# A held weight load, two loads moved ahead, and a routing cut into smaller steps

## The chip, the cores and the metric

The kernel runs on one core of a Trainium2 chip. The metric is the device time of one execution in microseconds; several executions are taken and the median is given. The profile is of one execution.

## The reference: linear attention, then a top-1 mixture of experts

Eight batches of 576 tokens, eight heads of 64, are put through attention without a softmax; the 4608 rows of 512 that come out each go to one of eight experts:

```
kv  = einsum('bhsd,bhse->bhde', k, v)
out = einsum('bhsd,bhde->bhse', q, kv)
x   = out / rms(out) * g_norm                # rows of 512, N = 4608
e   = argmax(x @ w_gate)                     # one expert of 8 per row
y   = softmax(x @ w_gate)[e] * sigmoid(x @ w_output_gate)[e] * (relu(x @ w1[e]) @ w2[e])
```

Everything is float32. The kernel keeps that precision with two-part operands: each weight or activation is split into a rounded part (`whi`, `xT`, `hT` high) and a remainder (`wlo`, ...), and three matmuls take the place of one.

## The kernel before

**Stages.** Attention goes batch by batch: the state of a batch (`kvps`, from loads `ld<-kvm` in four chunks and `ld<-rem`), a projection (`kvTps`, `mps`), then tiles of 128 rows (`ops`). The first sixteen tiles are made in `early()`; the rest in `late()`, a generator whose pieces are run between the matmuls of the experts. Tiles are routed in four groups of 9, 7, 10 and 10 (`route()`): scales, argmax, a count of the rows before each row, and tables of row numbers (`tblps`, added up in `tacc`).

**Experts.** After the second group each expert has a table of its first 256 rows, and GpSimd gathers them (`xg`, the rows, and `tl`, their scales). `run(i)` is one expert run: eight column blocks of the first matmul (`mm1`, tile `hps`, 12 matmuls each at 256 columns; block f+2 uses the PSUM buffer that ScalarE and VectorE have emptied of block f into `hT`), then two row tiles of the second (`mm2`, tile `yps`, 24 matmuls of 512 columns each). Seven such runs stand beside `late()`. The other rows are gathered for eight later runs, when all four groups are routed and the experts are ordered by size (`rows_of_all`, `epos`, `gidx`).

**Order.** Each engine's instructions stand in the order in which this program writes them (a manual schedule), so an instruction that waits holds back all behind it on its engine. SyncE issues nearly all loads: weights (`wload`, 512 KB each, tile `wraw`), attention inputs (512 KB each) and row writes (`xs<-xrow`). GpSimd issues the gathers and the output scatters. A DMA also waits until the one eight places before it, which used the same semaphore, has landed.

**At the end of `early()`.** The first chunk of the first expert's w1 was loaded earlier. The other three are held by a dependency (`behind`, L217 issues them): one until the first tail gather has landed, two until the second. Behind them on SyncE stand a row write, four chunks of w2 (held until VectorE has scaled the second gathered tile), and then the loads of the sixth batch.

**In `mm2` and `late()`.** `run()` gives out routing work in two ways: `unit`, one step of `late()` after each mm1 block and at one place of each mm2 tile, and `step()` at four more places of a tile. A step of `route()` is up to six instructions, or fewer up to a `yield 1`. Before a group's table matmuls of the third and fourth group three steps are let pass.

Of the kernel before, what the change touches and what calls it, by code (L numbers as in the profile page):

```python
# [11 lines left out]
F32 = mybir.dt.float32  # L12
# [9 lines left out]
P = 128  # L22
# [6 lines left out]
NT = NTOK // P  # L29
# [122 lines left out]
def body(ctx: ExitStack, tc: tile.TileContext, kvm, rem, qT, wg, gn, w1, w2, kc, xs, xr, xt, tab, out):  # L152
    nc = tc.nc
# [126 lines left out]
            out=o[:M, :], out_offset=None, in_=dram[0:XE] if i < E else dram,  # L280
            in_offset=bass.IndirectOffsetOnAxis(ap=gidx[i // E][:M, RUNS[i][0], t:t + 1], axis=0))

    issued = []

    def gather(i, after=None):
        for t, c0, M in tiles_of(i):
            xg[(i, t)] = take([P, DM], F32, "xg")
            x_ = fetch(i, t, M, xs, xg[(i, t)])
            if after is not None and t == tiles_of(i)[0][0]:
                tc.add_manual_dep(x_.ins, after.ins.name,  # L290
                                  mybir.DependencyInfo(mybir.DependencyClass.Sync, mybir.DependencyReason.DATA),
                                  reason="order of the gathers")
            gathered = gather_tail(i, t, M, xr if i < 2 else xt)
            issued.append(gathered)
        return gathered

    def tail_of(i, k, after=None, new=False):
# [23 lines left out]
    def behind(i_, after):  # L321
        if after is not None:
            tc.add_manual_dep(i_.ins, after.ins.name,
                              mybir.DependencyInfo(mybir.DependencyClass.Sync, mybir.DependencyReason.DATA),
                              reason="pace of the gathers")
        return i_
# [373 lines left out]
    def route(gi):  # L700
# [257 lines left out]
        yield from pause(8)  # L958
        if g0 >= EARLY:

            yield 1
            yield 1
            yield 1

        def table_part(t0, t1, rl=None):
            w = t1 - t0
# [13 lines left out]
        if not early:  # L980
            tps = ps_t.tile([P, 2, E * TMAX], F32, name="tblps", tag="t")
            for t in range(n):
                nc.tensor.matmul(tps, las[t], rc[:, t, 0:2], start=(t == 0), stop=(t == n - 1))
            yield from pause(9)
            vec.tensor_tensor(out=tacc, in0=tacc, in1=tps, op=ALU.add)
        elif not lead:
            tps, acc = table_part(0, TMAX)
            yield from pause(9)
            vec.tensor_copy(acc, tps)
            scales_late.append(rest_of_scales())  # L990
        else:
            tps, acc = table_part(0, TA, rl)
            yield from pause(9)
            vec.tensor_tensor(out=gidx[0][:, :, 0:TA], in0=acc, in1=tps, op=ALU.add)
            gather(0)
            vec.tensor_tensor(out=acc, in0=acc, in1=tps, op=ALU.add)
            for _ in places(0, tacc[:, 0].rearrange("p (e t) -> p e t", t=TMAX), 0, TA):
                pass
            ea = sm.tile([P, E], F32, name="ea", bufs=1)
            vec.tensor_tensor(out=ea, in0=cf[:, K_A:K_A + E], in1=rp[:, n], op=ALU.subtract)  # L1000
            ab_ = c1.tile([P, E], BF16, name="adj")
            vec.tensor_scalar(out=ab_, in0=ea, scalar1=0.0, scalar2=None, op0=ALU.max)
            adj.append(ab_)
            for _ in tokens_so_far():
                pass
            tick[0] = None

            scales_late.append(rest_of_scales())

            def others():  # L1010
                for k in range(3):
                    marks(TA, TMAX, k)
                    yield
                tps, acc = table_part(TA, TMAX)
                yield
                vec.tensor_tensor(out=acc, in0=acc, in1=tps, op=ALU.add)

            tables_late.append(others())
# [2 lines left out]
            yield from rows_of_all()  # L1021

    scales_late, tables_late = [], []
    xwrites = []
    opened = [False]

# [29 lines left out]
                if k == 2:  # L1056
                    routing.remove(r)

    def step(n=6):

        while n and routing:
            n -= 1
            k = next(routing[0], 2)
            if k == 2:
                routing.pop(0)
            if k:
                break
# [13 lines left out]
    def early():  # L1081

        nonlocal done_tiles

        def more():
            load(loads, free)
            if not loads and not opened[0]:
                open_rows()

        w1s = list(range(4))  # L1090

        def send(n=0):
            load(early_extra[:1] and [early_extra.pop(0)], free) if n else wload(0, 1, w1s.pop(0))

        more()
        for b in range(FIRST_B - 1):
            lim = min(tiles_ready(b - 1) if b else 0, EARLY)
            kv = kv_part(b)
            for k in range(4):
                next(kv)  # L1100
                more()
                if lim - done_tiles > 2:
                    run_out(lim)
            cp = next(kv)
            more()
            if not run_out(lim):
                constants(COLD[2])
            kvT = kvT_part(cp)
            if not run_out(lim) or b == FIRST_B - 2:
                constants(COLD[2])  # L1110
            m_part(b, kvT)
            if b == FIRST_B - 2:
                constants(COLD[5])
            more()
            while run_out(lim):
                more()

        while squares:
            sums()
        lim = tiles_ready(FIRST_B - 2)  # L1120
        kv = kv_part(FIRST_B - 1)
        assert not loads
        send()
        run_out(lim)
        constants(1)
        send(1)
        send(1)
        run_out(lim)
        for k in range(4):
            next(kv)  # L1130
            if k < 3:
                advance()
            if k == 1:
                run_out(lim)
                send(1)
                send(1)
        cp = next(kv)
        advance()
        kvT = kvT_part(cp)
        evict = out_tile(done_tiles, True)  # L1140
        done_tiles += 1
        m_part(FIRST_B - 1, kvT)
        evict()
        if len(squares) > 2:
            sums()
        advance()
        constants(COLD[2])
        assert done_tiles == lim
        run_out(EARLY)
        paced[0] = False  # L1150
        while run_out(EARLY):
            constants(1)
        constants(COLD[5])
        for r in rows:
            r()
        while squares:
            constants(COLD[2], sums())
        while routing:
            advance()
            if routing and COLD[3][at_pause[0]]:  # L1160
                constants(COLD[3][at_pause[0]], tick[0])
        while early_extra:
            send(1)
        for c in w1s:
            behind(wload(0, 1, c), issued[0] if c == 1 else issued[1])
        for k in range(PIECES):
            next(rest)
        constants(COLD[4], tick[0])
# [261 lines left out]
    with tc.manual_schedule(engines=MAN):  # L1430
# [24 lines left out]
            run(i, lambda n: next(rest, None))  # L1455
        for _ in rest:
            assert False
    p1.close()
    rp_[1] = main.enter_context(tc.tile_pool(name="rb", bufs=1))
    hp = main.enter_context(tc.tile_pool(name="hp", reuse_waits="tile", bufs=1))  # L1460
# [113 lines left out]
```

## Time and profile before

| | us |
|---|---|
| median of three runs (lowest, highest) | 589.47 (588.39, 592.59) |
| profiled execution | 589.1 |
| span of its trace | 587.3 |

The span reaches from the first to the last instruction of the trace; the profiled execution took 1.8 us more. TensorE (PE) is busy for 556.2 us of the span. A share of busy time is an average over stages with different limits, so the stages have to be read one by one: where PE waits, for whom, and what that one waited for. Engines are PE (matmul), PEld (its weight loads), DVE (VectorE), ACT (ScalarE), POOL (GpSimd) and SPq (SyncE's queue).

### The profile page before, as it was taken

Reading aid. Unit: us, or ns where it says so; the run is one execution under the profiler, and the core shown is the slowest. Engines: PE = TensorE matmul, PEld = TensorE weight load, DVE = VectorE, ACT = ScalarE, POOL = GpSimd, SP = SyncE. Lnnn points to the kernel's source line nnn. Section 1 sums busy time; section 2 is a strip of 40 time slices with the busy share of each in tenths; the row PEclk is TensorE's granted clock in tenths of the full one; section 3 lists DMA queues with packets and bytes.
Section 4 is the critical chain, followed back from the end, with each engine's and each line's share of the span. In section 5 each row is a group of like instructions: output and inputs, shape, how many; then the busy total and the mean of one; then the engine's idle time right before and its main releaser. Section 6 shows DMA issues by size and latency. Waiting matters only on the chain.

```text
span 587.3 us, 11846 instructions
## 1 busy us (share of the span) xinstructions
PE 556.2 (95%) x4626; PEld 476.4 (81%) x4626; DVE 345.1 (59%) x634; ACT 285.8 (49%) x482; POOL 217.2 (37%) x202
## 2 busy tenths in 40 slices
PE   7898769999999979999999999999999999999995
PEld 3774658898988778889989879889897988888894
DVE  2268574655587999757595737446345363656450
ACT  1354445656576637456563534435445353535430
POOL 3342333331313241524484515325263443545202
PEclk9999999999999999999999999999999999999998
DMA  8999599798967572865857436346554654656201
GB/s 305 408 410 337 160 393 406 286 353 285 317 216 246 176 269 67 304 230 178 283 155 250 129 122 185 111 155 189 166 168 141 199 155 153 199 168 205 74 6 37
DMA packets 38586, 126.18 MB, mean 215 GB/s; under 512 B 6877, under 2 KB 8142, under 8 KB 38528
## 3 DMA queue, kind: packets, MB, share of 16 engines
q1 hardware_dynamic: 29520, 105.19, 52.1%
q0 software_dynamic: 8288, 19.82, 10.1%
q8 instruction: 38, 0.62, 0.4%
q10 hardware_dynamic: 720, 0.38, 0.2%
q14 instruction: 20, 0.16, 0.1%
HBM read 106.01 MB, written 19.91 MB: 214 GB/s over the span
## 4 chain that ended last, share of the span: by engine, by line
PE 77%; DMA 8%; DVE 7%; ACT 3%; issue 3%; POOL 1%; SPq 0%; POOLq 0%; ACTq 0%; DVEq 0%
PE hps L389 33%; PE yps L425 30%; PE ops L644 4%; DMA ld<-kvm 4%; PE kvps L565 3%; PE tps L345 3%; PE yps L419 3%; DVE wlo L263 2%; ACT whi L260 1%; DMA wgs<-wg 1%; DMA wraw<-w 1%; DVE wlo L256 1%; PE cps L540 1%; DMA tl<-xr,gidx 1%; DVE la L897 0%
## 5 line engine op out<-in xcount | busy, mean ns | idle before, releaser
L389 PE MATMUL hps<-xT,whi 128*128 128x256 f32 (+8 forms) x1008 | 218.2, 309 | 6.0 <-DVE hT L399 5.2
L425 PE MATMUL yps<-whi,hT 128*128 128x512 f32 (+3 forms) x592 | 199.1, 400 | 0.0
L389 PEld LDWEIGHTS hps<-xT,whi 128*128 128x128 f32 x1008 | 167.1, 190 | 12.0 <-DVE hT L399 6.0
L389 PE MATMUL hps<-xT,wlo 128*128 128x256 f32 (+8 forms) x504 | 153.4, 304 | 0.0
L425 PEld LDWEIGHTS yps<-whi,hT 128*128 128x128 f32 (+3 forms) x592 | 110.1, 186 | 24.0
L397 ACT ACTIVATE hT<-hps 128x256 fp32r<-128x256 f32 (+8 forms) x128 | 55.0, 430 | 127.1 <-PE hps L389 124.6
L425 PE MATMUL yps<-wlo,hT 128*128 128x512 f32 (+3 forms) x296 | 116.0, 392 | 0.0
L399 DVE SCALAR_TENSOR_TENSOR hT<-hps,hT 128x256 fp32r<-128x256 f32 (+9 forms) x168 | 63.0, 395 | 88.8 <-ACT hT L397 88.4
L438 POOL DMA_INDIRECT out<-y,oidx x42 | 47.2, 1124 | 181.5 <-ACT y L437 153.4
L256 DVE SCALAR_TENSOR_TENSOR wlo<-wraw,gcol,whi 128x1024 fp32r<-128x1024 f32 x62 | 83.3, 1345 | 46.3 <-ACT whi L253 46.2
L263 DVE TENSOR_TENSOR wlo<-wraw,whi 128x1024 fp32r<-128x1024 f32 x64 | 85.1, 1330 | 28.0 <-ACT whi L260 26.5
L389 PEld LDWEIGHTS hps<-xT,wlo 128*128 128x128 f32 x504 | 95.9, 190 | 0.3
L253 ACT ACTIVATE whi<-wraw,gcol 128x1024 fp32r<-128x1024 f32 x62 | 71.3, 1150 | 0.7 <-DVE wlo L263 0.7
L279 POOL DMA_INDIRECT xg<-xs,gidx x42 | 47.1, 1121 | 57.3 <-PE hps L389 38.3
L260 ACT CAST whi<-wraw 128x1024 fp32r<-128x1024 f32 x64 | 66.6, 1040 | 1.9 <-issue 1.9
L279 POOL DMA_INDIRECT tl<-xt,gidx x42 | 54.1, 1288 | 30.0 <-PE hps L389 21.4
L425 PEld LDWEIGHTS yps<-wlo,hT 128*128 128x128 f32 (+3 forms) x296 | 55.2, 186 | 10.4
L315 POOL TENSOR_TENSOR xg<-xg,tl 128x512 f32<-128x512 f32 (+8 forms) x40 | 42.9, 1071 | 51.0 <-DMA tl<-xt,gidx 42.5
L437 ACT ACTIVATE y<-yps,tl 128x512 f32<-128x512 f32 (+3 forms) x37 | 25.4, 688 | 59.9 <-PE yps L425 47.9
L348 ACT CAST xT<-tps 128x512 fp32r<-128x512 f32 (+8 forms) x42 | 23.0, 547 | 39.4 <-PE tps L345 38.4
L349 DVE TENSOR_TENSOR xT<-tps,xT 128x512 fp32r<-128x512 f32 (+8 forms) x42 | 26.8, 637 | 19.3 <-ACT xT L348 19.0
L565 PEld LDWEIGHTS kvps<-ld 128*64 128x64 f32 (+1 forms) x640 | 21.8, 139 | 15.4 <-DMA ld<-kvm 7.4
(175 smaller groups left out, 442.3 us busy)
## 6 DMA issues: line engine op xcount, KB each, us to landing
wraw<-w SPq DMA_DIRECT2D x128, 512.0 KB, 4.5
ld<-kvm SPq DMA_DIRECT2D x32, 512.0 KB, 9.7
ld<-qT SPq DMA_DIRECT2D x18, 512.0 KB, 9.0
xs<-xrow SPq DMA_DIRECT2D x18, 512.0 KB, 4.3
ld<-rem SPq DMA_DIRECT2D x4, 512.0 KB, 7.9
xg<-xs,gidx POOLq DMA_INDIRECT x42, 4.1
tl<-xt,gidx POOLq DMA_INDIRECT x42, 4.7
out<-y,oidx POOLq DMA_INDIRECT x42, 3.3
```

Source lines behind the costliest of these rows:

```text
L253: he.activation(hi, r, AF.Copy, scale=gcol[:, 0:1])
L256: eng.scalar_tensor_tensor(out=lo, in0=r, scalar=gcol[:, 0:1], in1=hi.bitcast(F32), op0=ALU.mult, op1=ALU.subtract)
L260: he.copy(hi, r)
L263: eng.tensor_tensor(out=lo, in0=r, in1=hi.bitcast(F32), op=ALU.subtract)
L279: return nc.gpsimd.indirect_dma_start(out=o[:M, :], out_offset=None, in_=dram[0:XE] if i < E else dram, in_offset=bass.IndirectOffsetOnAxi ...
L315: return eng.tensor_tensor(out=v, in0=v, in1=f, op=ALU.mult)
L389: seq.append(nc.tensor.matmul(ps[:, :C], w[:, o:o + P], x[d][:, :C], start=(d == 0 and k == 0), stop=(d == 3 and k == 2)))
L397: nc.scalar.activation(h[:, 0:C], ps[:, :C], AF.Relu)
L399: nc.vector.scalar_tensor_tensor(out=h[:, l:l + b - a], in0=ps[:, a:b], scalar=0.0, in1=h[:, a:b].bitcast(F32), op0=ALU.max, op1=ALU.subtract)
L425: seq.append(nc.tensor.matmul(ps[:M], a, b, start=(f == 0 and n == 0), stop=(f == 7 and n == 2)))
L438: i_ = nc.gpsimd.indirect_dma_start(out=out, out_offset=bass.IndirectOffsetOnAxis(ap=oidx[i // E][:M, RUNS[i][0], t:t + 1], axis=0), in_=y ...
L565: nc.tensor.matmul(ps[u * D:(u + 1) * D, p * D:(p + 1) * D], k, v, start=(s == 0 and p == 0), stop=(s == 4 and p == NP - 1))
```

## The change

Three things. The second and third chunk of the first expert's w1 are no longer held; the fourth waits for a one-column memset that GpSimd executes behind its four gather instructions, so for their issue and not for their landing. Two loads of the sixth batch go out right behind it. And routing is spread: once all tiles are made and only the last group is being routed, a step has at most three instructions, and the third group's table comes two steps later.

```diff
@@ in route()
         if g0 >= EARLY:
 
-            yield 1
-            yield 1
-            yield 1
+            for _ in range(5 if not last else 3):
+                yield 1
...
             gather(0)
+            issued.append(nc.gpsimd.memset(issue_mark, 0.0))
...
-    def step(n=6):
-
+    def step():
+
+        n = 3 if done_tiles == NT and len(routing) == 1 and not squares else 6
         while n and routing:
...
@@ in early()
         while early_extra:
             send(1)
-        for c in w1s:
-            behind(wload(0, 1, c), issued[0] if c == 1 else issued[1])
+        for c in w1s[:-1]:
+            wload(0, 1, c)
+        behind(wload(0, 1, w1s[-1]), issued[0])
+        assert len(xfree) > 2
+        load([late_loads.pop(0) for _ in range(2)], xfree)
```

**SyncE, at the end of `early()`.** `wraw<-w` is a chunk of expert weights, `ld<-kvm` a chunk of keys and values; in brackets stand the semaphores that a row waits for (DMAHW: another load, DMASW: a gather, Pool: GpSimd). Before:

```order
L530 DMA ld<-kvm 128x1024 [waits DMAHW4_49,PE_49]
L530 DMA ld<-rem 128x1024 [waits DMAHW5_49,PE_49]
L217 DMA wraw<-w 128x1024 [waits DMAHW6_49,DMASW4_49,PE_49]
L217 DMA wraw<-w 128x1024 [waits DMAHW7_49,DMASW6_49,PE_49]
L217 DMA wraw<-w 128x1024 [waits DMAHW0_49,PE_49]
L1031 DMA xs<-xrow 128x1024 [waits DMAHW1_49,Activation_49]
L217 DMA wraw<-w 128x1024 [waits DMAHW2_49,DVE_49,PE_49]
```

Now:

```order
L528 DMA ld<-kvm 128x1024 [waits DMAHW4_49,PE_49]
L528 DMA ld<-rem 128x1024 [waits DMAHW5_49,PE_49]
L217 DMA wraw<-w 128x1024 [waits DMAHW6_49,PE_49]
L217 DMA wraw<-w 128x1024 [waits DMAHW7_49,PE_49]
L217 DMA wraw<-w 128x1024 [waits DMAHW0_49,PE_49,Pool_49]
L528 DMA ld<-kvm 128x1024 [waits DMAHW1_49]
L528 DMA ld<-kvm 128x1024 [waits DMAHW2_49]
L1031 DMA xs<-xrow 128x1024 [waits DMAHW3_49,Activation_49]
L217 DMA wraw<-w 128x1024 [waits DMAHW4_49,DVE_49,PE_49]
```

The two waits for gathers are gone, one for GpSimd is new, and two loads have come from behind the w2 chunks to in front of them. The semaphores of all later loads shift by two places with them: the sixth batch's third and fourth chunk had to wait for the first and second w2 chunk (DMAHW2, DMAHW3), and now wait for its second chunk and the row write.

**VectorE, in the mm1 of the fifth expert run.** `hT` is VectorE's part of emptying a block, `wlo` the split of a w2 chunk, the others are routing of the last group (`tacc`: the third group's table). From the first block's `hT`, before:

```order
L399 SCALAR_TENSOR_TENSOR hT<-hps,hT 128x256 [waits Activation_49]
L734 SCALAR_TENSOR_TENSOR ru<-ry 128x80 [waits DVE_49]
L736 TENSOR_TENSOR ru<-ru,ss 128x80 [waits DVE_49]
L738 SCALAR_TENSOR_TENSOR xtail<-ru,ry 128x10x8 [waits DVE_49]
L399 SCALAR_TENSOR_TENSOR hT<-hps,hT 128x256 [waits Activation_49]
L263 TENSOR_TENSOR wlo<-wraw,whi 128x1024 [waits DMAHW3_49,Activation_49]
L749 TENSOR_TENSOR gp<-gp,xtail 128x10x64 [waits DVE_49]
L749 TENSOR_TENSOR gp<-gp,xtail 128x10x64
L399 SCALAR_TENSOR_TENSOR hT<-hps,hT 128x256 [waits Activation_49]
```

Now:

```order
L397 SCALAR_TENSOR_TENSOR hT<-hps,hT 128x256 [waits Activation_49]
L982 TENSOR_TENSOR tacc<-tacc,tblps 128x96 [waits PE_49]
L397 SCALAR_TENSOR_TENSOR hT<-hps,hT 128x256 [waits Activation_49]
L263 TENSOR_TENSOR wlo<-wraw,whi 128x1024 [waits DMAHW3_49,Activation_49]
L717 TENSOR_SCALAR ry<-ss 128x80
L724 SCALAR_TENSOR_TENSOR ru<-ry 128x80 [waits DVE_49]
L726 TENSOR_TENSOR ru<-ru,ss 128x80 [waits DVE_49]
L397 SCALAR_TENSOR_TENSOR hT<-hps,hT 128x256 [waits Activation_49]
L728 SCALAR_TENSOR_TENSOR ru<-ru 128x80 [waits DVE_49]
L730 SCALAR_TENSOR_TENSOR ry<-ru,ry 128x80 [waits DVE_49]
L397 SCALAR_TENSOR_TENSOR hT<-hps,hT 128x256 [waits Activation_49]
```

Eight small instructions of the last group that stood ahead of the second block's `hT` stand two to three ahead of each, and the rest of that group's work comes later by as much; its argmax (`ohb`), which stood ahead of the fifth block's `hT`, now stands ahead of the eighth's.

**PE, second row tile of the fourth expert run.** `tps` are transposes of gathered rows, `tblps` the third group's table, each of its matmuls on a freshly loaded `la`. Before:

```order
L345 MATMUL tps<-ident,xg 128x128 x3
L425 MATMUL yps<-whi,hT 128x512
L425 MATMUL yps<-wlo,hT 128x512
L425 MATMUL yps<-whi,hT 128x512
L983 LDWEIGHTS la [waits DVE_49]
L983 MATMUL tblps<-rrc,la 128x96 [waits PE_49]
```

Now, from the `yps` behind the transposes:

```order
L423 MATMUL yps<-whi,hT 128x512
L423 MATMUL yps<-wlo,hT 128x512
L423 MATMUL yps<-whi,hT 128x512 x2
L423 MATMUL yps<-wlo,hT 128x512
L423 MATMUL yps<-whi,hT 128x512 x2
L423 MATMUL yps<-wlo,hT 128x512
L423 MATMUL yps<-whi,hT 128x512 x2
L423 MATMUL yps<-wlo,hT 128x512
L423 MATMUL yps<-whi,hT 128x512 x2
L423 MATMUL yps<-wlo,hT 128x512
L423 MATMUL yps<-whi,hT 128x512
L980 LDWEIGHTS la [waits DVE_49]
```

The table has moved behind twelve matmuls of the tile, to its end. The last group's table moved likewise, from the fifth run's second row tile into the sixth run's mm1.

## Rows read from the trace of the kernel before

**Rows 1.** the page's head; then by stage: stretch, engines' busy time, PEclk, DMA share, GB/s

```profile
span 587.3 us, 11846 instructions
...
56.00:66.00 10.00, 8.31 (x168) 5.41 (x166) 6.03 (x29) 3.04 (x7) 5.05 (x6) 1.00 0.52 145
78.00:94.00 16.00, 10.64 (x154) 9.45 (x153) 10.83 (x27) 7.75 (x17) 3.77 (x4) 0.89 1.03 407
94.00:176.00 82.00, 82.00 (x1010) 70.64 (x1008) 50.78 (x80) 51.76 (x95) 25.13 (x22) 1.00 0.84 304
200.00:245.00 45.00, 38.84 (x271) 34.23 (x271) 41.42 (x104) 23.40 (x41) 15.66 (x13) 1.00 0.57 195
```

**Rows 2.** PE's waits, 56 to 94 us: engine, line, awaited, us in total, times, longest

```profile
PE kvps L565 <- DMA ld<-kvm: 3.4, 3, 2.5
PE mps L595 <- ACT kvT L585: 2.0, 1, 2.0
PE tps L345 <- DVE xg L315: 0.5, 1, 0.5
```

**Rows 3.** the chain that ended last, 60 to 125 us (start, us, what)

```profile
65.31 4.79 DMA tl<-xr,gidx
...
72.57 7.38 DMA wraw<-w
...
80.01 12.86 DMA ld<-kvm
```

**Rows 4.** SyncE's DMA issues in order of time (start, us, what)

```profile
55.52 0.38 SPq L530 DMA_DIRECT2D ld<-kvm  x1
...
65.45 5.65 SPq L217 DMA_DIRECT2D wraw<-w  x3
```

**Rows 5.** GpSimd, then VectorE, around the first gathers

```profile
62.78 0.97 POOL L279 DMA_INDIRECT tl<-xr,gidx  x1 [0.30 <-issue]
...
65.47 0.69 DVE L315 TENSOR_TENSOR xg<-xg,tl 128x512 f32<-128x512 f32 x1 [2.68 <-DMA tl<-xr,gidx]
```

**Rows 6.** ScalarE and VectorE from 78 to 88 us

```profile
78.76 1.04 ACT L260 CAST whi<-wraw 128x1024 fp32r<-128x1024 f32 x1 [1.95 <-issue]
79.71 0.37 ACT L585 COPY kvT<-kvTps 128x256 f32<-128x256 f32 x1
...
79.83 1.23 DVE L263 TENSOR_TENSOR wlo<-wraw,whi 128x1024 fp32r<-128x1024 f32 x1 [2.56 <-ACT whi L260]
...
83.46 0.42 DVE L399 SCALAR_TENSOR_TENSOR hT<-hps,hT 128x256 fp32r<-128x256 f32 x1
...
87.28 0.42 DVE L399 SCALAR_TENSOR_TENSOR hT<-hps,hT 128x256 fp32r<-128x256 f32 x1
```

**Rows 7.** PE's matmul blocks at either clock

```profile
86.90 0.80 PE L389 MATMUL hps<-xT,whi 128*128 128x256 f32 x2
...
90.19 0.51 PE L389 MATMUL hps<-xT,whi 128*128 128x256 f32 x2
```

**Rows 8.** PE's waits, 170 to 262 us

```profile
PE hps L389 <- DVE hT L399: 4.8, 3, 2.0
PE tblps L983 <- DVE la L897: 1.4, 2, 1.2
```

**Rows 9.** PE in the fifth and sixth run, with the idle time before

```profile
214.83 0.51 PE L389 MATMUL hps<-xT,whi 128*128 128x256 f32 x2 [1.60 <-DVE hT L399]
...
220.09 0.50 PE L389 MATMUL hps<-xT,whi 128*128 128x256 f32 x2 [1.96 <-DVE hT L399]
...
243.60 0.51 PE L389 MATMUL hps<-xT,whi 128*128 128x256 f32 x2 [1.20 <-DVE hT L399]
```

**Rows 10.** VectorE, then GpSimd, in the last routing

```profile
212.88 1.56 DVE L749 TENSOR_TENSOR gp<-gp,xtail 128x640 f32<-128x640 f32 x2
...
217.97 1.73 DVE L779 TENSOR_TENSOR ohb<-rsc,rsx 128x80 bf16<-128x80 f32 x1
...
218.54 1.05 POOL L315 TENSOR_TENSOR xg<-xg,tl 128x512 f32<-128x512 f32 x1
```

More of the change, by code (lines that the diff above doesn't have):

```diff
@@ L281, in fetch @@
             in_offset=bass.IndirectOffsetOnAxis(ap=gidx[i // E][:M, RUNS[i][0], t:t + 1], axis=0))
-    issued = []
     def gather(i, after=None):
@@ L293, in gather @@
             gathered = gather_tail(i, t, M, xr if i < 2 else xt)
-            issued.append(gathered)
         return gathered
@@ L1023, in body @@
     scales_late, tables_late = [], []
+    issued = []
+    issue_mark = c1.tile([P, 1], F32, name="issue_mark")
     xwrites = []
@@ L1457, in body @@
             assert False
+        assert not routing
     p1.close()
```

## The prediction

> **What bounds the kernel now.** I read the page's head first, then busy time by stage. From 94 to 176 us PE is busy without a break; from 78 to 94 it is busy for 10.64 of 16 us, and from 200 to 245 for 38.84 of 45 [rows 1]. So the change can pay in two stretches: at the start of the expert runs and in the last routing.
>
> The first stretch I read in PE's waits, then in the chain. PE waits 3.4 us for attention loads (three waits, the longest 2.5), 2.0 for ScalarE's `kvT`, and 0.5 for the second gathered tile [rows 2]. The chain says what those loads waited for: the tail gather issued at 65.31, landed 4.79 us later; then a w2 chunk issued at 72.57, 7.38 us under way; then the sixth batch's fourth chunk, issued at 80.01 as that w2 chunk had landed, itself 12.86 us under way [rows 3]. The reader should see a queue that starts late: SyncE issues a load at 55.52 (and one more behind it), and weights not before 65.45, held by the first tail [rows 4]. The DMA engines have a busy share of 0.52 from 56 to 66, and of 1.03 from 78 to 94 [rows 1]. `kvT` was late for the same reason: on ScalarE it stands behind the rounding of the first w2 chunk, which began at 78.76 [rows 6].
>
> The second stretch is VectorE's: it is busy 41.42 of 45 us [rows 1]. PE waits 4.8 us for `hT` (three times) and 1.4 for `la`, of which 1.2 at once [rows 8]. The three `hT` waits are 1.60 and 1.96 in the fifth run and 1.20 in the sixth [rows 9]; behind the first stand two `gp` of 1.56 us together, behind the second an `ohb` of 1.73 [rows 10].
>
> **The front stretch: what goes.** The two freed loads leave right behind those of 55.52, by about 57, some 9 us earlier than now, while half the DMA engines' time is free. The marker stands behind GpSimd's fourth gather instruction; that one starts at 65.31 [rows 3], and its like takes 0.97 [rows 5], so the fourth load leaves at about 66.4 and the two attention loads by 67.3. The memset itself I cost at nothing more: one column, and GpSimd has nothing to do behind it but gathers that wait for PE.
>
> Then I count transfers of 512 KB. Now five (two w1, a row write, two w2) take 9.8 us from the first one's issue at 70.1, when the tail has landed, to the landing at 79.95. Eight more and two gathers take the 12.9 us to 92.87 [rows 3]. In the changed order five (one w1, two attention, the row write, the first w2) start at 66.4, so the first w2 chunk lands at about 76.2; seven more, at eight's pace or a little under, bring the fourth attention chunk at about 87.5. Rounding and `kvT` come 2.5 us earlier than at 78.76 and 79.71 [rows 6]: PE's 2.0 us go. The first two attention chunks are now third from the front: of their 3.4 us 3.0 go, and up to 0.4 for the fourth chunk may stay, or go too. The second tile's transposes are then limited by PE's own work: 0.5. Sum 5.5 to 5.9; I take 5.9.
>
> The clock: from 78 to 94 the granted share is 0.89 [rows 1], that is 3.5 us at the lower of its two levels (1.2 GHz), in a stretch that PE fills to two thirds. Two matmuls took 0.80 us there and 0.51 at 2.4 GHz [rows 7]. 3.5 us at half speed lose 1.76; at 0.67 busy that costs 1.2. With the waits gone I expect no such fall. Together 7.1 us.
>
> **What comes back.** VectorE is late next. From the first w2 remainder (79.83) to the third block's `hT` (83.46) lie 3.6 us of routing of the first two groups, and the fourth block's `hT` follows 3.8 later [rows 6]. The remainder can now start at 77.3, so the third block is emptied at 81.3 (its `hT` takes 0.4) and the fourth at 85.1. PE would start the fifth block at 80.8: 86.90 [rows 7] less the 5.5 of waits ahead of it and 0.6 of the lost clock. It would start the sixth about 2.4 later than it may start the fifth (3.29 between 86.90 and 90.19 [rows 7], less the rest of the lost clock), at 83.7. New waits: 0.5 and 1.4. Net 7.1 less 1.9, **5.2 us**; the count of transfers gives the same for the fourth chunk (92.87 to 87.5). Bounds: 7.1 if VectorE gets through sooner, about 3 if a tail lands late. From 94 to 176 PE waits for nothing, and loads and matmuls shift alike, so I cost that stretch at nothing; its cover is gone if loads there turn out to have less than those 5 us in hand.
>
> **The last routing.** The third group's table waits 1.2 us inside a tile; twelve matmuls later its `la` are there. I keep 0.8 of it, since VectorE's work up to there is in the unchanged order and holds the next run's first block. In the fifth run the waits of 1.60 and 1.96 stood behind much routing at a time. Now at most three instructions stand ahead of an `hT`, but the two `gp` still fall together, and a w2 split (1.23 in [rows 6]) is due in every second block. Stepping down VectorE's new list with the durations of the trace, I get waits of 1.0, 0.2 and 0.4 to 1.0: 1.9 gained of 3.56. In the sixth run the 1.20 turns into 1.1 at the first eviction, where VectorE's backlog ends; the tables' move gives 0.3. Sum 3.1, taken as **3.0 us**. Bounds: nothing, if the backlog only changes place; 5, if nearly all of it passes into the time behind 245 us. The middle is argued from [rows 1]: VectorE has 3.6 us free in 45, so what PE gains has to be put off, and the steps that make `epos` and `gidx` are, by 5 to 10 us. The later runs that need these are gathered 40 us on: cost nothing.
>
> **Sum.** 589.1 (the profiled execution: a span of 587.3 [rows 1] and 1.8 around it) less 5.2 less 3.0: **580.9 us**. The median of the runs, 589.5, is 0.4 above that execution, which is within what the terms leave open.
>
> **Rivals.**
>
> *VectorE keeps the second gain* (0.18). For it: `ohb`, which started at 217.97, ended at 219.70, as GpSimd's scaling (218.54, 1.05 us) ended [rows 10]. If both scalings of the fifth run fall on work ahead of an eviction, 2.1 of the 3.0 us come back. Against: the old order had such a hit too, so part of it is in the 3.56. 589.1 less 5.2 less 0.9: 583.0. The Trainium skill's page "SBUF — State Buffer" (Terms) says that VectorE and GpSimd share a port pair as an exclusive lock, held for a whole instruction, while the loser blocks fully. The `ohb` agrees with it.
>
> *The freed loads slow the gathers* (0.12). For it: the first tail had released VectorE 2.7 us after its issue (62.78, 65.47), the second took 4.79, with a weight load issued at 65.45 beside it [rows 3 to 5]. Now two loads precede the first tail and three follow the second; 2.1 us on either delay all behind it. Against: the load behind starts a microsecond after the tail, not 0.1, and the two ahead should have landed by 64. 589.1 less 3.1 less 3.0: 583.0. The Trainium skill's page "DMA: Bandwidth & Descriptors" (Queues, rings and completion order) says that each DMA engine goes round the queues that have work, a packet at a time; by that rule a gather beside loads is slowed, which speaks against taking the hold away.
>
> *The loads don't leave early* (0.05). They also wait for PE to have read their buffers' old contents. That should be over by 52 us, but no row shows it. If not, the queue starts at about 65.5 and some 2 us are missing: 583.
>
> *Gathers starve* (0.04), the other side. Were the first tail as slow as the slowest transfer, 12.86 instead of 2.7 us, PE's start would slip by 10.2; the waits that are removed take up 5.2 of it, and 5.0 are left: 594.1, or 591.1 with the routing's gain. It decides against the change once the slip exceeds 8.2 us.
>
> *Both in full* (0.04): 589.1 less 7.1 less 5.0: 577.0.
>
> **Numbers.** My forecast has 0.57, at 580.9, with a range of its own from 579 to 583. The 8 in 10 take in the two rivals at 583.0, both of them together (586), and the full gain: 577.0 to 586.0. One per cent, about what a measurement of this kernel can tell from no change, is 5.9 us, so the line is 583.6 from the median; the cases at 583 lie just beyond it, and I split them. Faster 0.77, within 0.18, slower 0.05.
>
> **What would show it.** Right: weight loads at 56 to 57 us, and at 66.4; no wait for `kvT`, under 0.5 us for attention loads up to 94 us, no fall of the clock there; two new `hT` waits between 80 and 86; the fourth chunk's landing some 5 us earlier; then PE without a break. In the routing: no wait at the third group's table, `hT` waits of the fifth run together near 1.7, one near 1 at the start of the sixth. Wrong: a tail that lands 2 us later than now, `hT` waits from 200 to 255 us with the old sum, or waits for loads between 94 and 176.

## The result, and the profile after

The changed kernel takes **581.5 us** (median, 581.2 to 582.5) where the kernel before takes 588.9 beside it: a ratio of 0.987, interval 0.982 to 0.992. The forecast was 580.9. The span went from 587.3 to 579.3 us, and two marks split these 8.0 us. The second matmul of the first run (the first `yps` row) begins at 93.82 instead of 98.09: the front gave 4.3 us, against a forecast of 5.2. From the start of the fourth run to that of the seventh takes 81.76 us instead of 85.37: the last routing gave 3.6, forecast 3.0. Neither gain was handed back. A few executions of the later runs were slow ones (one took 908 us, one 1874), and all medians and ratios leave those out.

Busy time by stage, in the columns of [rows 1]:

```profile
56.00:66.00 10.00, 8.30 (x169) 5.41 (x166) 5.83 (x29) 2.99 (x7) 5.00 (x6) 1.00 0.77 251
78.00:94.00 16.00, 12.99 (x221) 11.78 (x222) 12.58 (x30) 9.61 (x23) 4.73 (x5) 1.00 1.03 407
94.00:176.00 82.00, 82.00 (x1011) 70.73 (x1011) 52.57 (x86) 51.05 (x94) 26.31 (x24) 1.00 0.83 297
200.00:245.00 45.00, 42.48 (x306) 37.90 (x305) 38.87 (x86) 25.65 (x46) 19.19 (x15) 1.00 0.64 220
```

In the first line the DMA engines are busy for 0.77 instead of 0.52: the freed loads. In the second PE works 12.99 us instead of 10.64 and the clock stays at 2.4 GHz. The third is still full. In the last PE is busy for 3.6 us more, and VectorE, 41.42 us before [rows 1], is no longer busier than PE. SyncE's issues (start, duration, what), to hold against [rows 4]:

```profile
56.52 10.25 SPq L217 DMA_DIRECT2D wraw<-w  x3
66.82 0.90 SPq L528 DMA_DIRECT2D ld<-kvm  x2
...
69.30 2.77 SPq L217 DMA_DIRECT2D wraw<-w  x4
...
74.28 2.22 SPq L528 DMA_DIRECT2D ld<-kvm  x2
```

Three weight loads stand in the first row; it spans 10.25 us because the third, the held one, left at 66.44. The attention loads follow at 66.82 and the first w2 chunk at 69.30. PE's waits from 56 to 94 us, against [rows 2]:

```profile
PE hps L387 <- DVE hT L397: 2.1, 2, 1.5
...
PE mps L593 <- ACT kvT L583: 1.1, 1, 1.1
...
PE tps L343 <- DVE xg L313: 0.2, 1, 0.2
```

No wait for attention loads is left. The wait for `kvT` is halved, and two new ones for VectorE's `hT` stand there. The same in PE's timeline, with the idle time in brackets:

```profile
78.88 0.30 PE L593 MATMUL mps<-gw,kvT 64*64 64x16 f32 x8 [1.14 <-ACT kvT L583]
...
82.69 0.39 PE L387 MATMUL hps<-xT,whi 128*128 128x256 f32 x1 [0.68 <-DVE hT L397]
...
86.55 0.38 PE L387 MATMUL hps<-xT,whi 128*128 128x256 f32 x1 [1.45 <-DVE hT L397]
...
88.17 0.45 PE L563 MATMUL kvps<-ld 128*64 128x64 f32 x7
```

The last row is the fourth attention chunk, 12.86 us under way before [rows 3]. It lands at 88.08 and is taken up 0.1 us later without a wait: the queue and VectorE now end together. ScalarE and VectorE, against [rows 6]:

```profile
77.51 1.04 ACT L260 CAST whi<-wraw 128x1024 fp32r<-128x1024 f32 x1 [1.13 <-DMA wraw<-w]
78.46 0.36 ACT L583 COPY kvT<-kvTps 128x256 f32<-128x256 f32 x1
...
78.58 1.23 DVE L263 TENSOR_TENSOR wlo<-wraw,whi 128x1024 fp32r<-128x1024 f32 x1 [1.75 <-ACT whi L260]
...
82.22 0.42 DVE L397 SCALAR_TENSOR_TENSOR hT<-hps,hT 128x256 fp32r<-128x256 f32 x1
...
86.07 0.42 DVE L397 SCALAR_TENSOR_TENSOR hT<-hps,hT 128x256 fp32r<-128x256 f32 x1
```

All of it comes 1.2 us earlier than before, and the distances from the remainder to the two `hT` (3.6 and 3.9) are the old ones, as the forecast took them. PE's waits from 170 to 262 us, against [rows 8]:

```profile
PE hps L387 <- DVE xT L347: 1.3, 2, 0.7
PE hps L387 <- DVE hT L397: 1.1, 2, 0.8
```

4.8 and 1.4 us have become 2.4; PE waits for no table.

### The profile page after: what moved, and what is told of

It is laid out like the page before. It is cut to its first block, busy times and chain, and to the rows that moved or that the text cites. A ratio compares the mean times of both kernels' runs of the same rounds, so it can differ in the third digit from the quotient of the medians.

```text
span 579.3 us, 11842 instructions
## 1 busy us (share of the span) xinstructions
PE 555.1 (96%) x4626; PEld 475.4 (82%) x4626; DVE 345.7 (60%) x634; ACT 285.4 (49%) x482; POOL 221.2 (38%) x203
## 4 chain that ended last, share of the span: by engine, by line
PE 78%; DVE 10%; DMA 5%; issue 3%; ACT 3%; POOL 1%; POOLq 0%; ACTq 0%; DVEq 0%; SPq 0%
PE hps L387 33%; PE yps L423 31%; PE ops L642 4%; PE tps L343 3%; PE kvps L563 3%; PE yps L417 3%; DVE wlo L263 2%; DMA ld<-kvm 1%; DMA wgs<-wg 1%; DMA wraw<-w 1%; ACT whi L260 1%; DVE wlo L256 1%; PE cps L538 1%; DVE hT L397 1%; DVE la L895 1%
## 5 line engine op out<-in xcount | busy, mean ns | idle before, releaser
L436 POOL DMA_INDIRECT out<-y,oidx x42 | 48.7, 1160 | 173.7 <-ACT y L435 145.1
L397 DVE SCALAR_TENSOR_TENSOR hT<-hps,hT 128x256 fp32r<-128x256 f32 (+9 forms) x168 | 62.9, 395 | 86.0 <-ACT hT L395 85.6
L260 ACT CAST whi<-wraw 128x1024 fp32r<-128x1024 f32 x64 | 66.6, 1040 | 1.1 <-DMA wraw<-w 1.1
L279 POOL DMA_INDIRECT tl<-xt,gidx x42 | 55.3, 1316 | 28.6 <-PE hps L387 21.1
L642 PE MATMUL ops<-aug,ld 64*64 64x80 f32 (+1 forms) x960 | 32.2, 244 | 1.4 <-ACT gp L673 1.3
```

What stands on the lines that cost most here:

```text
L260: he.copy(hi, r)
L279: return nc.gpsimd.indirect_dma_start(out=o[:M, :], out_offset=None, in_=dram[0:XE] if i < E else dram, in_offset=bass.IndirectOffsetOnAxi ...
L397: nc.vector.scalar_tensor_tensor(out=h[:, l:l + b - a], in0=ps[:, a:b], scalar=0.0, in1=h[:, a:b].bitcast(F32), op0=ALU.max, op1=ALU.subtract)
L436: i_ = nc.gpsimd.indirect_dma_start(out=out, out_offset=bass.IndirectOffsetOnAxis(ap=oidx[i // E][:M, RUNS[i][0], t:t + 1], axis=0), in_=y ...
L642: nc.tensor.matmul(ps[c0:c0 + step_, u, p * W:(p + 1) * W], qt[g // 2][r, p, q0:q0 + step_], augs[b % 3][r, p, :], start=True, stop=True)
```

## The experiments

They ran on three chips, four kernels on each. A trace has three marks: where the runs begin (first `hps` row), where the first run's second matmul begins (first `yps` row), and the time from the fourth run's start to the seventh's. "Pauses" are short halts of PE between 63 and 67.5 us, told of below. Times in us; the ratio is to the kernel before on the same chip, whose medians were 592.2 (A), 594.2 (B) and 590.7 (C).

| run | chip | pauses | runs begin | second matmul | 4th to 7th run | median | ratio (95%) |
|---|---|---|---|---|---|---|---|
| before | first | no | 67.55 | 98.09 | 85.37 | 588.9 | |
| after | first | no | 67.80 | 93.82 | 81.76 | 581.5 | 0.987 (0.982 to 0.992) |
| front only | A | yes | 73.17 | 98.34 | 87.15 | 590.6 | 0.995 (0.991 to 0.998) |
| routing only | A | yes | 71.51 | 97.82 | 82.33 | 587.2 | 0.989 (0.984 to 0.994) |
| loads not ahead | A | yes | 73.78 | 98.54 | 82.33 | 586.5 | 0.988 (0.983 to 0.993) |
| no hold | A | yes | 72.49 | 96.81 | 81.98 | 585.0 | 0.985 (0.980 to 0.990) |
| before again | B | yes | 73.13 | 98.58 | 87.14 | 590.8 | 0.996 (0.993 to 1.000) |
| after again | B | yes | 73.68 | 98.01 | 82.45 | 586.3 | 0.989 (0.981 to 0.997) |
| scales late | B | yes | 74.38 | 103.06 | 82.01 | 584.6 | 0.985 (0.975 to 0.996) |
| no hold, scales late | B | yes | 73.88 | 96.97 | 82.14 | 584.8 | 0.986 (0.981 to 0.990) |
| after, third | C | no | 67.35 | 93.25 | 81.95 | 581.8 | 0.987 (0.983 to 0.992) |
| steps of three | C | no | 67.94 | 94.48 | 84.89 | 583.6 | 0.989 (0.985 to 0.994) |
| five yields | C | no | 67.91 | 94.30 | 84.14 | 584.7 | 0.992 (0.989 to 0.996) |
| scales late again | C | no | 69.21 | 94.44 | 81.79 | 581.7 | 0.987 (0.983 to 0.992) |

The kernel before came out at 0.996 against itself on chip B, with an interval that ends just short of 1: differences under half a per cent are therefore read from the marks, not from these ratios.

**Front only**, edit against the changed kernel:

```diff
-            for _ in range(5 if not last else 3):
+            for _ in range(3):
...
-        n = 3 if done_tiles == NT and len(routing) == 1 and not squares else 6
+        n = 6
```

> The change with its routing part undone: steps of six everywhere, three yields ahead of the tables in every group. Theory (the two parts stand in stretches of their own and add up): the front's 4.3 us as the second matmul of the first run began earlier (98.09 to 93.82) and nothing of the routing's 3.6: a span of 583.0, 584.6 against 588.9. PE would wait again 1.6, 2.0 and 1.2 us for hT and about 1.2 for the table between 170 and 262 us. Rival (the front moves loads and VectorE's work that the last routing then profits from): part of the 3.6 comes with the front, 581 to 583.

**Routing only**, edit against the kernel before:

```diff
-            yield 1
-            yield 1
-            yield 1
+            for _ in range(5 if not last else 3):
+                yield 1
...
+        n = 3 if done_tiles == NT and len(routing) == 1 and not squares else 6
```

> The kernel before with the routing part alone: steps of three in the last group, five yields ahead of the tables. Theory: 3.6 us, 585.3 against 588.9, a span of 583.7; up to 176 us its trace is that of before (second matmul of the first run at 98.1), and the waits of PE for hT between 200 and 262 fall from 4.8 to about 2.4 with none for the table. Rival (the gain needs the earlier front): under 1 us, 588 to 589.

The routing part needs no earlier front: 82.33 us from the fourth to the seventh run, and PE's waits from 170 to 262 us are those of the changed kernel. Routing only:

```profile
PE hps L389 <- DVE xT L349: 1.3, 2, 0.8
PE hps L389 <- DVE hT L399: 1.1, 2, 0.8
```

The front alone did not give its 4.3 us, and neither theory had foreseen why: the runs began at 73.17, and the second matmul at 98.34, no earlier than in the kernel before on chip B (98.58) and later than with the old front on its own chip (routing only, 97.82). Nor did it give anything to the last routing: 87.15 us, with PE's waits for `hT` (4.8) and for the table (1.4) back whole. The next two runs were made to see whether that lies in the kernel.

**Before again** and **after again**: no edit.

> The kernel before, word for word, for its trace on the chip that the next runs share. In the four runs ahead of this one TensorE stopped for 0.4 us after every few small matmuls between 63 and 67.5 us and began the expert runs at 71.5 to 73.8 us, while the two traces of the first comparison began at 67.6 and 67.8. If that belongs to the chip or to the execution, it is here as well where it is in the other three runs, the second matmul of the first run begins at 97.8 to 98.5 as in the run with the routing part alone, and the median is about 592; on a chip without it 98.1 and 589. Rival (it comes with how these kernels differ): none of it here, with it in the next three.

> The changed kernel, word for word, on the same chip. Without the 0.4 us stops: runs from 67.8, second matmul of the first run at 93.8, 7.4 us below the kernel before. With them (theory: a late start eats the front's gain, since the loads that PE waited for in the kernel before have landed by then anyway): runs from 72 to 73.5, second matmul at 97 to 98.5, about what the kernel before has there, and 3.6 us or a little more below it, from the last routing alone.

PE's timeline of the changed kernel on chip B:

```profile
63.49 0.35 PE L642 MATMUL ops<-aug,ld 64*64 64x80 f32 x4 [0.45 <-issue]
64.23 0.39 PE L642 MATMUL ops<-aug,ld 64*64 64x80 f32 x5 [0.39 <-issue]
64.98 0.37 PE L642 MATMUL ops<-aug,ld 64*64 64x80 f32 x5 [0.37 <-issue]
65.73 0.53 PE L642 MATMUL ops<-aug,ld 64*64 64x80 f32 x3 [0.38 <-issue]
...
67.18 1.88 PE L563 MATMUL kvps<-ld 128*64 128x64 f32 x30 [0.51 <-issue]
...
73.68 0.55 PE L369 MATMUL hps<-xT,whi 128*128 128x128 f32 x3 [0.68 <-ACT xT L346]
```

And of the kernel before on chip B:

```profile
65.32 0.38 PE L644 MATMUL ops<-aug,ld 64*64 64x80 f32 x5 [0.32 <-issue]
66.08 0.35 PE L565 MATMUL kvps<-ld 128*64 128x64 f32 x5 [0.37 <-issue]
67.52 1.28 PE L565 MATMUL kvps<-ld 128*64 128x64 f32 x27 [1.09 <-issue]
...
73.13 0.66 PE L371 MATMUL hps<-xT,whi 128*128 128x128 f32 x4 [0.68 <-ACT xT L348]
```

PE does three to five small matmuls, halts for 0.3 to 0.5 us (once 1.1), and goes on; "issue" means that it waited for nothing that the profile shows. Both kernels do it on A and B, in all eight traces, and neither on C or in the first comparison. So it goes with the chip (or the hour), not with the change. The halts that the profile names add up to 1.8 to 2.5 us, and the granted clock falls behind them in most of these traces: routing only, whose clock stayed up there, begins its runs at 71.51; the two with 3.4 us of the lower clock begin at 72.49 and 73.17, the five with 6.8 us at 73.13 to 74.38 (before again has half of it ahead of the halts).

In the kernel before the runs begin 5.6 us later on chip B, while the second attention chunk is taken up only 0.4 us later (86.20 instead of 85.84). So PE waits 0.6 us for attention loads there instead of 3.4, and the front has little to give: 98.58 to 98.01. (Both traces have 6.8 us of the lower clock near 61 to 72 us, so the 0.6 is rough.) The theory for this case is borne out by these marks, but it is half of the account: the changed kernel's own queue is late as well. SyncE's waits from 60 to 80 us, changed kernel, chip B:

```profile
SPq L217 <- DVE xg L313: 3.6, 1, 3.6
SPq L1031 <- ACT xrow L651: 3.2, 1, 3.2
```

In the first comparison the first of these was 1.0 us and the second was missing. The data of the row write and VectorE's scaling of the second tile stand behind PE's late matmuls, SyncE stands behind both, and the first w2 chunk leaves at 75.05 instead of 69.30, no earlier than in the kernel before on that chip (74.47). A late start of PE thus takes away the lead that the front gives to the w2 chunks.

In the last routing the two differ by 4.7 us on chip B, not 3.6. Stage 200 to 245 of the kernel before there shows where the rest is:

```profile
200.00:245.00 45.00, 40.05 (x266) 35.26 (x264) 39.83 (x98) 22.51 (x39) 14.42 (x12) 0.96 0.51 179
```

The clock is at its lower level (1.2 GHz) for 3.4 us from 221.8, just behind the wait of 1.96. The same happened with front only (from 222.0) and not in the first trace of the kernel before. The long waits thus had a second price that is paid in some executions: in three of the four traces that have the wait of 1.96.

**Loads not ahead**:

```diff
-        assert len(xfree) > 2
-        load([late_loads.pop(0) for _ in range(2)], xfree)
```

> The change without the sixth batch's two loads ahead of the second weights: they go out at their old place behind them. Theory (the queue's total sets the end: the fourth attention chunk lands at 88.1 whatever the order ahead of it, and the move only chooses which wait is paid): the first w2 chunk lands some 3 to 4 us earlier than 78.7 and the 1.1 us wait for kvT goes; the first attention chunk lands at 81 to 83 instead of 72.4 and PE waits 1 to 2 us for it at 80; the second matmul of the first run begins at 93.8 to 94.8, so 581.5 to 582.5. Rival (first attention chunk is the binding one, as in the kernel before, where it took 2.5 us): 2 to 3 us slower than the change, 583.5 to 584.5. Second rival (the kvT wait is the binding one): 1 us faster than the change, 580.5.

The second matmul began at 98.54 on chip A, against 98.01 for the change on chip B, from starts at 73.78 and 73.68: 0.4 us lost. PE waited 0.2 us for attention loads and not at all for `kvT`. That rules out the 2 to 3 us of the first rival under a late start; how it stands with a start at 67.8 was not run.

**No hold**:

```diff
-        behind(wload(0, 1, w1s[-1]), issued[0])
+        wload(0, 1, w1s[-1])
```

> The change without the hold on the fourth weight load: it does not wait for GpSimd's marker, so it and the two attention loads leave at about 57.4 instead of 66.4 us. Theory (the tails are not slowed by loads that are already under way, as the first tail's release at 65.7 against 65.5 showed): first w2 chunk lands at 74 to 75 instead of 78.7, kvT's wait of 1.1 us goes, VectorE's remainders start earlier, the front gives 0.5 to 1.1 us more: 580.4 to 581.0. Rival (loads beside a gather slow it): the first tail, issued at 65.35, releases VectorE 2 us later than at 65.7, PE's first run starts at 69.5 to 70 instead of 67.8, and 1 to 2 us of the front's gain are lost: 582.5 to 583.5.

Here the rival's mechanism showed. All three weight loads leave at once, and two attention loads behind them. SyncE, no hold:

```profile
56.32 1.61 SPq L217 DMA_DIRECT2D wraw<-w  x3
58.05 1.02 SPq L528 DMA_DIRECT2D ld<-kvm  x2
```

VectorE, no hold, and then the changed kernel:

```profile
68.71 0.69 DVE L313 TENSOR_TENSOR xg<-xg,tl 128x512 f32<-128x512 f32 x1 [6.14 <-DMA tl<-xr,gidx]
```

```profile
65.72 0.69 DVE L313 TENSOR_TENSOR xg<-xg,tl 128x512 f32<-128x512 f32 x1 [2.87 <-DMA tl<-xr,gidx]
```

The first tail releases VectorE 3 us later. The other run without the hold shows the same (6.30), and in the twelve traces with a hold or with the old front this wait is 2.65 to 3.06 us. On chip A it stayed hidden, since PE was at the small matmuls ahead of the first tile until 70.05 us and reached the tile at 71.22 (585.0 us, the lowest of the four there; the change itself was not run on A). In the first comparison PE waited 0.17 us for that tile at 66.47 already, so with a start at 67.8 the 3 us should stand in the open; that was not run. The Trainium skill's page "DMA: Bandwidth & Descriptors" (Queues, rings and completion order) says that each DMA engine goes round the queues that have work, a packet at a time. The forecast took from it that a gather beside loads is slowed; this trace agrees, with 6.14 us against 2.87.

**Scales late**, and again on chip C:

```diff
-                if 1 <= f <= 3:
+                if f in (2, 4, 5):
```

> The change with the routing scales of the first two groups taken up behind the third, fifth and sixth block of the first run's first matmul instead of the second to fourth. Theory (the fourth attention chunk's landing at 88.1 binds that stretch, since PE took it up 0.1 us later with no wait): the hT waits of 0.68 and 1.45 us go and come back as a wait for that chunk or as a later scale; the second matmul begins within 0.4 us of 93.8, the time within 0.5 of the change. Rival (VectorE binds): 1.5 to 2.1 us faster than the change. A price that could show: the first run's tail gathers start later and its second tiles wait for them at 101.

> The change with the two early groups' scales behind the third, fifth and sixth block, run again since the clock was at its lower level for 13.7 us from 76.9 in the execution traced before. Theory (the loads bind the stretch and the scales only choose where PE waits): within 0.5 us of the changed kernel. Rival (with the loads early enough VectorE binds): hT waits of the front down from 1.4 to 2.1 to 0.6 or less, the second matmul of the first run 1 to 1.5 us earlier against its start than in the changed kernel (24.3 to 26.0 us), and 1 to 1.5 us faster.

The run on B tells little: its executions lie between 582.0 and 590.6 us, and its trace has the lower clock for 6.8 us from 66.6 and for 13.7 from 76.9. On C, PE's timeline shows both halves of the theory:

```profile
86.27 0.50 PE L387 MATMUL hps<-xT,whi 128*128 128x256 f32 x2 [0.49 <-DVE hT L397]
...
89.27 0.69 PE L563 MATMUL kvps<-ld 128*64 128x64 f32 x16 [0.70 <-DMA ld<-kvm]
```

The `hT` waits fell from 2.1 to 0.5 us, and 0.7 came back as a wait for the fourth attention chunk, 0.05 us after that landed. From the runs' start it is 25.2 us to the second matmul against 25.9 for the change on C, and the medians are 581.7 and 581.8. So 0.7 us came off that stretch, short of the rival's 1 to 1.5, and nothing off the time, as the theory had it. The pair is not a clean one: 3.4 us of the lower clock from 61.4 put the start off to 69.21 and, by way of the second tile, the first w2 chunk to 70.58 (67.35 and 68.72 in the third trace of the change). With that said, the two limits stand side by side.

**No hold, scales late**: both edits above.

> Both: no hold on the fourth weight load, and the scales later. Theory (two limits stand side by side, the queue and VectorE, and only both together move the end): the fourth load and two attention loads leave at 57 instead of 66.4, all behind land some 3 us earlier, and the scales are out of the way: the second matmul of the first run begins 2 to 3 us earlier than in the change, 579 on a chip with a start at 67.8. Rival (the early loads hold up the gathers): the runs begin 1 to 2 us later than in the change and the sum is nothing.

From start to second matmul it takes 23.1 us instead of the change's 24.3 on that chip, each with the lower clock for 6.8 us: 1.2 gained, half of what was expected. The median is 1.5 us below, which the intervals don't separate. No version that beats the change is shown.

**After, third**: no edit. **Steps of three** and **five yields**:

```diff
-            for _ in range(5 if not last else 3):
+            for _ in range(3):
```

```diff
-        n = 3 if done_tiles == NT and len(routing) == 1 and not squares else 6
+        n = 6
```

> The changed kernel once more, as partner of the next three. From the start of the fourth run's first matmul to the end of the seventh's it took 81.8 and 82.4 us in the two traces so far, 85.4 in the kernel before. If TensorE's stops between 63 and 67.5 us are there again, runs begin at 72 to 74 and the time is 584 to 587; without them 67.8 and 581.5.

(The mark is the seventh run's start, not its end; the numbers are right.)

> The change with the third group's tables left at three yields: the steps of three alone are kept of the routing part. Theory (as forecast, the table's place is worth about 0.8 to 1.1 and the steps the rest): PE waits 1.2 us for the table again and no other wait shrinks; the stretch from the fourth run to the seventh takes 82.6 to 83.2 us, the time is 0.8 to 1.2 above the changed kernel. Rival (the table's wait is taken by VectorE's own backlog, and the later tables only pass it on): the stretch stays at 81.8 to 82.1.

> The change with steps of six in the last routing: the tables' later place alone is kept. Theory: the hT waits of 1.60, 1.96 and 1.20 come back nearly whole, the table's wait of 1.2 stays away; the stretch takes 84.2 to 84.6 us, the time is 2.4 to 2.8 above the changed kernel, more if the clock falls behind those waits as it did at 222 us in two executions with them. Rival (the two edits only work together, since the backlog passes from one to the other): 85.4, nothing left of the gain.

PE's waits from 170 to 262 us, steps of three, then five yields:

```profile
PE hps L387 <- DVE hT L397: 3.1, 3, 2.0
PE tblps L980 <- DVE la L895: 1.2, 1, 1.2
```

```profile
PE hps L387 <- DVE hT L397: 3.1, 4, 1.3
...
PE tblps L980 <- DVE la L895: 0.6, 1, 0.6
PE hps L387 <- DVE xT L347: 0.6, 1, 0.6
```

Five yields alone take 84.14 us, next to the 84.2 to 84.6 expected; the 1.60, 1.96 and 1.20 became 1.34, 0.84, 0.65 and 0.26 rather than coming back whole, and a table wait of 0.6 came with them. Steps of three alone miss: 84.89 us, though 1.2 of that is the clock at its lower level for 3.4 us from 215.9, behind a wait of 1.96 again (PE is busy for 79.85 us of the stretch, against 78.69 in the third trace of the change). Without it some 83.7 are left. Against the 85.37 of neither edit and the 81.8 of both, the yields alone give 1.2 and the steps alone about 1.6; together 3.6. PE's idle time (the stretch less its busy time) says it more plainly: 6.84 us with neither edit, 5.04 with either, 3.20 with both. The edits add up.

The wait of 1.96 that the steps alone leave standing is not quite the old one. VectorE and GpSimd, steps of three:

```profile
214.35 1.15 DVE L764 TENSOR_TENSOR rd<-lg,mx 128x80 f32<-128x80 f32 x1
...
214.34 1.05 POOL L313 TENSOR_TENSOR xg<-xg,tl 128x512 f32<-128x512 f32 x1
```

The `rd` takes 0.24 us elsewhere. The 0.9 that it lost beside GpSimd's scaling stand right ahead of the `hT` that PE waits for. In the kernel before the `ohb` of 1.73 [rows 10] lost 1.5 in the same way (it takes 0.24 in the changed kernel), in all three traces of that order.

## Why the prediction was right

**The front, 5.2 forecast, 4.3 measured.** The steps happened in the forecast's order; the sizes were these.

| term (us) | forecast | measured |
|---|---|---|
| waits for loads, `kvT`, second tile gone | 5.9 | 4.7 |
| clock at 2.4 GHz throughout | 1.2 | 1.9 |
| new `hT` waits | -1.9 | -2.1 |
| later start | 0 | -0.2 |
| sum | 5.2 | 4.3 |

The measured terms are PE's idle time between the runs' start and the second matmul (7.05 us before, 4.47 after) and its busy time there (23.49 and 21.55). The step that was mis-sized is the count of transfers. Five were to take 9.8 us from 66.4 and land the first w2 chunk at 76.2. The chunk released ScalarE at 77.51, after 11.1 us, so 1.14 of the 2.0 us for `kvT` stayed. The second tile's gathers were still under way when those five began (its `xg` landed at 67.42); in the kernel before all gathers had landed by 70.1, where the 9.8 us start. A second thing goes the same way: the sum let that chunk stand in the queue with the others, but it was held for VectorE's scaling of the second tile. SyncE waited 1.0 us for it and issued the chunk at 69.30, 2.9 us behind the first of the five, where the fifth left 2.4 us behind the first in the kernel before (72.57 and 70.16). On chip C it left 2.7 and, with the scales late, 3.7 us behind, and landed after 10.8 and 12.0. What share either has was not separated. The clock's term was too small: while the clock was low, from 85.6 to 89.0, PE was busy for 3.17 of 3.41 us, not for the stage's 0.67.

The `hT` waits came at 82.69 and 86.55, 0.68 and 1.45 where 0.5 and 1.4 were forecast. Of VectorE's list between, one `rdn` took 0.89 us where its like took 0.16 at 85.36, and it ended as GpSimd's scaling of a gathered tile ended. VectorE, then GpSimd:

```profile
83.86 0.89 DVE L817 TENSOR_SCALAR rdn<-rdn 128x7 f32<-128x7 f32 x1
...
82.76 1.97 POOL L313 TENSOR_TENSOR xg<-xg,tl 128x512 f32<-128x512 f32 x1 [0.62 <-DMA tl<-xr,gidx]
```

So that rival of the last routing shows in the front too, with 0.7 us. The forecast's distance of 3.8 between the two `hT` held since the old order had a loss of about that size there: a `wlo` of 1.92 us at 83.79, beside GpSimd's scaling at 83.59, against 1.28 now.

**The cover behind it held.** From 94 to 176 us PE is without a break, and the 4.3 us arrive unchanged at the fourth run (175.97 to 171.67).

**The last routing, 3.0 forecast, 3.6 measured.** The tables' 1.40 us went and 0.58 came for the first block: 0.8, where 0.8 and, for the tables' move, 0.3 were forecast. The sixth run's 1.20 became 0.68 and 0.29, a gain of 0.2 with 0.1 forecast. The fifth run's 3.56 became 0.79, a gain of 2.8 with 1.9 forecast: only the first of the three waits that were stepped down came about. Of the old 3.56, 1.5 were the `ohb`'s loss beside GpSimd, which in the new order falls where nobody waits. (The three gains come to 3.8; idle times too short for a row take 0.2 back.)

**The rivals.** VectorE's losses beside GpSimd's scaling fell on the fifth run as that rival had it. VectorE and GpSimd, the changed kernel:

```profile
213.63 2.00 DVE L263 TENSOR_TENSOR wlo<-wraw,whi 128x1024 fp32r<-128x1024 f32 x1
...
217.16 0.80 DVE L768 SCALAR_TENSOR_TENSOR rsc<-rd,cf 128x80 f32<-128x80 f32 x1
...
213.49 1.05 POOL L313 TENSOR_TENSOR xg<-xg,tl 128x512 f32<-128x512 f32 x1
...
216.81 1.04 POOL L313 TENSOR_TENSOR xg<-xg,tl 128x512 f32<-128x512 f32 x1 [2.27 <-DMA tl<-xt,gidx]
```

A `wlo` of 2.00 us (1.23 elsewhere) and an `rsc` of 0.80 (its neighbours of that size 0.24) lost some 1.3 us, but the `hT` behind them were in time, since at most three steps now stand ahead of each: PE waits nowhere there. The forecast did not choose where GpSimd's scaling falls. With steps of three alone it fell on the `rd` ahead of an awaited `hT`, so that it costs nothing in the changed kernel is luck as far as the runs show. The gathers were hardly slowed (2.87 us against 2.68), and the experiments without the hold show that the hold on the fourth load, and on the two loads behind it, is what keeps it so: the mechanism is real, its price at the gather 3 us, and the change steps round it. The loads did leave early, at 56.5.

**What the forecast left out**: that the front's gain rests on the runs beginning at 67.8. On chips A and B they begin at 71.5 to 74.4; on B the front gives 0.6 us and the change 4.5 (590.8 to 586.3), and 586.3 lies just beyond the wider range of the forecast, 577.0 to 586.0. That the first comparison met no halts is luck. So is part of the sum's closeness: the front fell 0.9 short and the routing gave 0.6 too much. The front alone was not run where the halts are absent; there its gain rests on the marks of the five traces with the new front (second matmul at 93.25 to 94.48 against 98.09).

## What to carry to other kernels

A wait that is removed from one queue pays until the next limit, so list both ends: here loads and VectorE end within 0.1 us of each other, and relieving VectorE alone gave nothing. Two loads issued 5 us ahead of a gather on the critical path cost it next to nothing (2.87 us against 2.68), though the second landed only at 63.99 in the third trace of the change, behind the issue of the first tail at 62.43; five cost it 3 us. Before a gain is booked as sure, ask which start time it assumes: a gain in load waits vanishes when something else delays the consumer, and here the loads held for the consumer's tiles were delayed with it.

## What the runs showed of the hardware

- In eight traces on two chips, both kernels alike, PE halted for 0.2 to 0.5 us (in three traces once for 0.8 to 1.1) after every few small matmuls between 63 and 67.5 us, 1.8 to 2.5 us in all, waiting for nothing that the profile shows; in six traces elsewhere it never did. A transfer of 16 KB on the instruction queue begins at 62.6 to 63.0 us in six of the eight, at 65.0 and 65.3 in the two without the hold, and at 62.3 to 63.2 in the other six, so the record of it doesn't tell them apart. GpSimd's four gathers are issued between 61.0 and 66.7 us in all. The cause stays open.
- In seven of the eight traces the granted clock fell, between 65.6 and 68.4 us, for 3.4 or 6.8 us; in three of the four traces with an `hT` wait of 1.96 us in the fifth run it fell behind that wait, for 3.4 us.
- The first tail gather, with five loads issued in the microseconds ahead of it instead of two, released its reader 6.1 and 6.3 us after VectorE began to wait, instead of 2.65 to 3.06.
- Short VectorE instructions that met GpSimd's scaling of a tile (`ohb`, `rd`, `rsc`, `rdn`) took 0.8 to 1.7 us instead of 0.2 and ended 0.02 to 0.11 us after it.
